# Another written-out issue order for a fused adaLN, sliding-window attention and GeGLU kernel

## The chip, the cores and the metric

The kernel runs on one core of a Trainium2 chip. Its time is device microseconds of one execution. Every engine of the core (PE for matmuls, DVE for elementwise work, ACT for activations and copies, POOL for small things, SP for issuing DMAs) has its own queue of instructions, works through it in order, and waits on semaphores for what other engines or transfers must deliver first.

## The reference, cut to what matters

The input x is 2048 rows of 512 bf16 values. Six vectors of 512 come from a conditioning vector c. They shift, scale and gate an attention layer and a feed-forward layer.

```python
mod = (silu(c) @ w_mod).reshape(1, 6, 1, 512)       # sa, ca, ga, sb, cb, gb
h = layernorm(x) * (1 + ca) + sa
x = x + ga * A(h, wqkv, wo)
h = layernorm(x) * (1 + cb) + sb
x = x + gb * (gelu(h @ w_gate) * (h @ w_up)) @ w_down    # w_gate, w_up: 512 x 1792
# A: 32 heads of 16; position s looks at s, s-2, ..., s-14 (8 places, masked below 0)
#    logits = q . k / 4, softmax over the 8 places, o = sum of attn * v, then o @ wo
```

## The kernel before, in words

**Groups.** The 2048 rows are worked on in four groups of 512 (called 0 to 3). For a group the steps are:

- LN1: statistics on DVE (L408, `bn_stats`) or ACT (L386 to L397), the inverse root on POOL (L445), the normalised rows `xn` on DVE (L422). Then `xn` is transposed: on PE for groups 0 (L481, in two halves, `th0` and `th1`), 1 and 2 (L458), by one DMA for group 3 (L464, called LN1.3.t). ACT (L496, four instructions per group, LN1.g.h0 to h3) applies scale and shift and leaves `hT`.
- qkv: twelve projections qp.g.block.j of four matmuls each (L563, L545 for the first two of group 0), each into one of four `mm` buffers of PSUM. ACT copies each out (q L577, k L579, v L583), which makes the buffer free again.
- logits: DVE multiplies q with eight shifted views of k (L618, four `pq` tiles of 128x4096). PE sums over the head dimension with 32-column tiles (L632, lp.g.0, lp.g.1, ..., and lp.g for the last). DVE and ACT do the softmax (ACT's exp is L660). The weights are brought into the layout of v by PE (L690) in group 0, and by a DMA through DRAM in the others.
- v: its transpose goes to DRAM (L589, vst.g), and four loads (L598, V4.g.0 to V4.g.2 and V4ld.g) bring shifted copies. DVE multiplies them with the weights (L725, pv.g.j), PE sums (L739, 32-column tiles), ACT copies (L750), PE multiplies with wo (L760), DVE adds x (L769).
- LN2: as LN1. Group 0 is transposed by PE, the others by DMA.
- FFN: for 14 tiles of 128 features, PE computes gate and up (L788, `g` and `u`, four matmuls each), ACT applies gelu (L821, `gl`) and copies (L828, `ub`), DVE multiplies (L839, `hh`). Then PE multiplies with w_down (L800; L811 for the last 128 rows), DVE adds x (L846, L853), and SP stores the output.

Ahead of the groups stand loads, the conditioning vectors (L294, function `cols`: 16 matmuls with one moving column each; L347 in 32-column tiles for the two gates), and twenty "warm" matmuls (L211) of a tile of zeros into a PSUM buffer that nobody reads. The gates ga and gb are spread over all partitions by a small store and a load through DRAM (L308, L312), and are multiplied into wo and w_down.

**What sets the order.** Every step is a Python generator, called a thread; it yields one `Op` after another: an engine, and a function that emits the instructions of this op. 111 threads are spawned. A list `ORDER` at the top of the file (L19 on) holds 846 thread numbers, and `Issuer.run` goes through it and emits the next op of the thread named:

```python
nxt = [next(g, None) for g in self.threads]
for i in ORDER:
    op = nxt[i]
    assert all(name in self.done for name in op.after), (op.fire, op.after)
    ...
    op.fn()
    ...
    nxt[i] = next(self.threads[i], None)
```

The list thus sets the order of every engine's queue: 276 ops on PE, 219 on DVE, 256 on ACT, 12 on POOL, 83 on SP. No scheduler changes it later (`tc.manual_schedule`). Within one thread the order is that of the code. The numbers `w` and `lat` in an `Op` are not read by `run`. Buffers come from pools (`mm` 4, `att` 2, `prod` 4, `hh` 16, and so on), and an op that takes a buffer waits on the chip until its last reader is done. Thread numbers: 0 constants, 1 to 4 loads, 5 and 6 the gates' way through DRAM, 7 and 9 to 11 the conditioning vectors, 8 the warm matmuls, 12 and 13 the gates into the weights, and from 15 on 24 per group (group 0: 15 to 38, group 1: 39 to 62, and so on; 14 is a second part of group 0's LN1).

All DMAs but two small early ones are issued by SP, and so lie on one queue.

Of the kernel before, what the change touches and what calls it, by code (L numbers as in the profile page):

```python
# [16 lines left out]
PT_DMA = (1, 2, 3)  # L17

ORDER = [  # L19
# [33 lines left out]
]  # L53


# [865 lines left out]
```

## Time and profile before

| | |
|---|---|
| median of 3 runs | 239.58 us (239.35 to 239.76) |
| span of the profiled execution | 237.6 us |
| the profiled execution's own time | not given by the page; the median lies 1.98 us above the span |
| PE, DVE, ACT busy | 231.6, 169.6, 150.7 us |
| granted PE clock | 1.00 in all stages looked at |
| DMA | 29.68 MB, 125 GB/s on average |

The span runs from the first instruction to the last. "Busy" counts the time in which an engine has an instruction under way; matmuls are pipelined, so a busy PE may still have small steps between its instructions. In a line of the timeline the first two numbers are start and length in us, then come the engine, the source line, the operation, output and input, and in brackets the idle time before it and who ended it. Source lines are those of the kernel before; the changed file is one line shorter above the functions, so its lines are lower by one.

### The profile page before, as it was taken

How to read it: one execution, taken by the hardware profiler on the slowest of the kernel's cores; microseconds unless marked ns; L12 is line 12 of the kernel's file. 1: busy time of each engine (PE TensorE's matmuls, PEld its weight loads, DVE VectorE, ACT ScalarE, POOL GpSimd, SP SyncE). 2: the span in 40 equal slices, each digit the busy share in tenths (PEclk: the TensorE clock that was granted, in tenths of full speed). 3: DMA queues.
4: the chain of work that ended last, by engine and by line, in shares of the span. 5: the costliest groups of instructions: out<-in, count | busy, mean ns of one | idle time of the engine just before them, and what ended most of it. 6: DMA issues, size and time to landing. Idle time of an engine off the chain costs nothing.

```text
span 237.6 us, 3691 instructions
## 1 busy us (share of the span) xinstructions
PE 231.6 (97%) x1403; PEld 109.1 (46%) x1403; DVE 169.6 (71%) x238; ACT 150.7 (63%) x287; POOL 12.4 (5%) x37
## 2 busy tenths in 40 slices
PE   7999899999999999999999999999999999999994
PEld 2656355544544444444444444444444444444443
DVE  3989999999999989999797899936742202322222
ACT  4689999977995756973775953552378560366300
POOL 1620101000100000010000010000100000000000
PEclk9999999999999999999999999999999999999999
DMA  6998896999967879307301977100080000100011
GB/s 213 349 306 237 219 202 162 205 356 308 193 163 211 263 181 196 59 3 177 90 0 43 206 158 136 44 22 0 22 91 1 0 22 25 44 0 0 0 47 44
DMA packets 35337, 29.68 MB, mean 125 GB/s; under 512 B 12664, under 2 KB 33784, under 8 KB 35320
## 3 DMA queue, kind: packets, MB, share of 16 engines
q1 hardware_dynamic: 35040, 29.19, 50.3%
q10 hardware_dynamic: 280, 0.26, 0.3%
q8 instruction: 11, 0.18, 0.3%
q14 instruction: 6, 0.05, 0.1%
HBM read 22.37 MB, written 4.98 MB: 115 GB/s over the span
## 4 chain that ended last, share of the span: by engine, by line
PE 87%; ACT 8%; DMA 2%; DVE 1%; issue 0%; POOL 0%; ACTq 0%
PE u_ps L788 21%; PE g_ps L788 20%; PE y_ps L800 19%; PE qkv_ps L563 12%; PE x_ps L760 6%; PE o_ps L739 3%; PE LTp L632 2%; DMA x<-in_A_x_dram 2%; ACT vT L583 2%; ACT gl L397 2%; ACT gl L386 2%; PE y_ps L811 1%; ACT hT L496 1%; PE qkv_ps L545 1%; ACT kT L579 1%; DVE st L408 1%
## 5 line engine op out<-in xcount | busy, mean ns | idle before, releaser
L788 PE MATMUL u_ps<-h,Wu 128*128 128x512 bf16 x224 | 57.6, 379 | 0.0
L788 PE MATMUL g_ps<-h,Wg 128*128 128x512 bf16 x224 | 57.5, 379 | 0.0
L821 ACT ACTIVATE gl<-g_ps 128x512 bf16<-128x512 f32 x56 | 33.7, 602 | 23.0 <-PE g_ps L788 20.8
L828 ACT CAST ub<-u_ps 128x512 bf16<-128x512 f32 x56 | 33.0, 588 | 22.6 <-PE u_ps L788 22.2
L800 PE MATMUL y_ps<-Wd,hht 128*128 128x512 bf16 x210 | 46.3, 379 | 0.0
L563 PE MATMUL qkv_ps<-hT,wqkv 128*128 128x512 bf16 x184 | 41.8, 380 | 0.6 <-ACT qT L577 0.6
L839 DVE TENSOR_TENSOR hht<-gl,ub 128x512 bf16<-128x512 bf16 x56 | 22.4, 423 | 27.1 <-ACT ub L828 27.1
L618 DVE TENSOR_TENSOR pq<-qT,kT 128x4096 bf16<-128x4096 bf16 x16 | 36.2, 2286 | 0.9 <-ACT kT L579 0.9
L725 DVE TENSOR_TENSOR pv<-PT,V 128x4096 bf16<-128x4096 bf16 x16 | 35.8, 2287 | 0.2 <-issue 0.2
L788 PEld LDWEIGHTS <-Wu 128*128 128x128 bf16 x224 | 21.4, 98 | 27.6 <-issue 2.5
L788 PEld LDWEIGHTS <-Wg 128*128 128x128 bf16 x224 | 21.7, 98 | 26.8 <-issue 1.0
L800 PEld LDWEIGHTS <-hht 128*128 128x128 bf16 x210 | 20.5, 98 | 24.8
L563 PEld LDWEIGHTS <-wqkv 128*128 128x128 bf16 x184 | 20.3, 114 | 20.3 <-issue 3.3
L846 DVE TENSOR_TENSOR ot<-y_ps,x 128x512 bf16<-128x512 f32 x15 | 10.1, 688 | 18.7 <-PE y_ps L800 18.7
L769 DVE TENSOR_TENSOR x<-x_ps,x 128x512 bf16<-128x512 f32 x16 | 10.6, 685 | 9.6 <-PE x_ps L760 9.6
L445 POOL TENSOR_TENSOR rstd<-rstd,neghalf 128x4 f32<-128x4 f32 (+1 forms) x9 | 8.6, 956 | 157.8 <-DVE rstd L439 87.3
L760 PE MATMUL x_ps<-woP,oT 128*128 128x512 bf16 x64 | 15.3, 379 | 0.0
L408 DVE BATCH_NORM_STATS2 st<-x 128x6 f32<-128x512 bf16 x19 | 12.8, 675 | 3.0 <-DMA x<-in_A_x_dram 3.0
L496 ACT ACTIVATE h<-h,modT,scl 128x512 bf16<-128x512 bf16 x12 | 8.9, 805 | 8.9 <-DMA h<-xn 8.9
L750 ACT CAST oT<-o_ps 128x512 bf16<-128x512 f32 x16 | 8.8, 591 | 7.5 <-PE o_ps L739 7.5
L579 ACT CAST kT<-qkv_ps 128x512 bf16<-128x512 f32 x16 | 9.8, 613 | 0.8 <-PE qkv_ps L563 0.8
L577 ACT CAST qT<-qkv_ps 128x512 bf16<-128x512 f32 x16 | 9.5, 604 | 0.5 <-PE qkv_ps L563 0.5
(78 smaller groups left out, 178.8 us busy)
## 6 DMA issues: line engine op xcount, KB each, us to landing
V<-vscr SPq DMA_DIRECT2D x12, 520.0 KB, 8.2
wm<-in_w_mod_dram SPq DMA_DIRECT2D x6, 512.0 KB, 4.8
vscr<-vT SPq DMA_DIRECT2D x4, 512.0 KB, 4.2
out_dram<-ot SPq DMA_DIRECT2D x15, 128.0 KB, 1.7
Wg<-in_B_w_gate_dram SPq DMA_DIRECT2D x1, 1792.0 KB, 8.9
Wu<-in_B_w_up_dram SPq DMA_DIRECT2D x1, 1792.0 KB, 12.3
wqkv<-in_A_wqkv_dram SPq DMA_DIRECT2D x3, 512.0 KB, 8.0
x<-in_A_x_dram SPq DMA_DIRECT2D x3, 512.0 KB, 9.0
```

The source lines that it names most:

```text
L408: nc.vector.bn_stats(out=st[:], in_=src()[:, c4, :])
L496: nc.scalar.activation(out=o, in_=B[key, dtp][:, :, dd, :] if pe else o, func=ACT.Identity, scale=sc(dt), bias=bi(dt))
L563: nc.tensor.matmul(ps[:], lhsT=wqkv[blk][:, dt, j::4], rhs=B["hT", sg][:, :, dt, :], start=(dt == 0), stop=(dt == DT - 1))
L579: nc.scalar.copy(out=kT[:, j, 16 + sg * SG:16 + (sg + 1) * SG], in_=ps[:])
L618: nc.vector.tensor_tensor(out=pq[:], in0=_ap(B["qT", sg][:, j, :], [[0, W], [1, SG]]), in1=_ap(kT[:, j, sg * SG + 2:sg * SG + 2 + SG], [[2 ...
L725: nc.vector.tensor_tensor(out=t[:], in0=_ap(B["PT", sg][:, 0, :], [[SG, 2], [0, 4], [1, SG]]), in1=_ap(v[:, 0, j, :], [[8, 2], [4 * (SG + ...
L760: nc.tensor.matmul(ps[:], lhsT=B["oT", sg][:, j, c4 * P:(c4 + 1) * P], rhs=woP[:, j, :], start=(j == 0), stop=(j == 3))
L788: nc.tensor.matmul(ps[:], lhsT=Wt[:, dt, ft * P:(ft + 1) * P], rhs=B["h2T", sg][:, :, dt, :], start=(dt == 0), stop=(dt == DT - 1))
L800: nc.tensor.matmul(ps[:], lhsT=B["hh", sg, ft][:, c4 * P:(c4 + 1) * P], rhs=B["Wd", ft // 4][:, ft % 4, :], start=(ft == 0), stop=(ft == F ...
L821: nc.scalar.activation(out=gl[:], in_=B["g", sg, ft][:], func=ACT.Gelu_apprx_tanh)
L828: nc.scalar.copy(out=ub[:], in_=B["u", sg, ft][:])
L839: nc.vector.tensor_tensor(out=hh[:], in0=B["gl", sg, ft][:], in1=B["ub", sg, ft][:], op=ALU.mult)
```

## The change

Only the list `ORDER` differs: 52 lines become 51, with the same 846 entries in another order. Each engine has the same ops as before, at other places in its queue. The diff begins so, and nothing outside the list is touched:

```diff
 ORDER = [
-    1, 1, 2, 2, 2, 0, 8, 8, 8, 8, 8, 17, 8, 8, 8, 8, 7, 7, 7, 7, 8, 8, 8, 8, 8, 8, 17, 17, 17, 17, 17, 17, 17,
-    17, 17, 17, 9, 17, 8, 8, 7, 7, 8, 8, 7, 7, 18, 18, 19, 19, 2, 2, 2, 2, 2, 19, 14, 14, 14, 14, 2, 2, 14, 8,
-    8, 39, 39, 39, 3, 3, 20, 20, 20, 20, 21, 21, 21, 21, 2, 2, 2, 20, 20, 20, 21, 21, 0, 0, 21, 20, 20, 20, 20,
...
+    0, 8, 8, 8, 8, 2, 17, 17, 8, 1, 1, 8, 0, 8, 17, 17, 17, 17, 8, 8, 17, 2, 2, 2, 2, 2, 2, 2, 2, 7, 7, 8, 8, 8,
+    8, 8, 7, 7, 7, 17, 17, 17, 18, 7, 7, 17, 17, 18, 7, 14, 19, 19, 0, 8, 8, 8, 8, 8, 19, 8, 8, 14, 14, 3, 3,
+    39, 39, 39, 14, 14, 2, 2, 20, 20, 20, 21, 9, 20, 41, 2, 21, 21, 20, 41, 41, 21, 21, 20, 20, 20, 20, 63, 63,
...
 ]
```

Read by engine, it moves these (before, then after):

```
PE, start:  16 warm, cols(1), 2 warm, cols(0), th0, th1, 2 warm, qph.0 (first projection)
            13 warm, cols(1), th0, cols(0), th1, 7 warm, qph.0
SP, middle: V4.0.0 V4.0.1 V4.0.2 vst.1 V4ld.0 LN1.3.t ga Wg vst.2 Wu V4.1.0
            V4.0.0 gst2 V4.0.1 V4.0.2 vst.1 ga V4ld.0 Wg LN1.3.t Wu vst.2 V4.1.0
SP, later:  pt.1.1 wm5 Wd0 Wd1 Wd2 Wd3 gst5 vst.3 gb V4.2.0
            pt.1.1 vst.3 wm5 Wd0 gst5 gb V4.2.0 Wd1 Wd2
```

In the logits sum of group 0, the last piece (lp.0) stands behind three projections of group 1 on PE, and the statistics of LN1.2 stand ahead of group 0's fourth product (L618) on DVE. The projections of group 1 come in the order in which ACT copies them out. Runs of 32-column tiles on PE are broken into 16 places where they were in 14. On PE the order from the fourth feature tile of the last group to the end is the same.

59 rows, old and new, of the table ORDER are left out of this document.

## The prediction

> **What bounds the kernel now.** The page's first part says which engine is full, its clock row whether it runs at full speed, the waits what TensorE (PE) still waits for.
>
> ```profile
> PE 231.6 (97%) x1403; PEld 109.1 (46%) x1403; DVE 169.6 (71%) x238; ACT 150.7 (63%) x287; POOL 12.4 (5%) x37
> PEclk9999999999999999999999999999999999999999
> PE 87%; ACT 8%; DMA 2%; DVE 1%; issue 0%; POOL 0%; ACTq 0%
> PE LTp L632 <- DVE pq L618: 0.8, 1, 0.8
> PE qkv_ps L563 <- ACT qT L577: 0.6, 2, 0.4
> ```
>
> PE is busy for 231.6 of 237.6 us. In the timeline its last wait of the body ends at 35.76 us; from there to the last projection it never stops. So a new order can gain only what PE loses before 35.76 (stalls, and stand-in "warm" matmuls ahead of the first real one), and loses whenever PE has to wait later. PE's timeline shows both places:
>
> ```profile
> 7.44 0.59 PE L211 MATMUL warm_ps<-gB 128*128 128x512 bf16 x2
> 8.41 1.89 PE L481 MATMUL hTp<-ident,xn 128*128 128x128 bf16 x16
> 10.13 0.59 PE L211 MATMUL warm_ps<-gB 128*128 128x512 bf16 x2
> 10.56 1.91 PE L545 MATMUL qkv_ps<-hT,wqkv 128*128 128x256 bf16 x16
> ...
> 25.17 0.61 PE L632 MATMUL LTp<-pq,Mph 128*32 128x512 bf16 x8 [0.78 <-DVE pq L618]
> 29.80 1.89 PE L563 MATMUL qkv_ps<-hT,wqkv 128*128 128x512 bf16 x8 [0.43 <-ACT qT L577]
> 35.76 2.75 PE L563 MATMUL qkv_ps<-hT,wqkv 128*128 128x512 bf16 x12 [0.18 <-ACT qT L577]
> ```
>
> Third, SP's timeline (which DMA is issued when) and the windows, for one stage where the change puts transfers in another order:
>
> ```profile
> 40.15 1.87 SPq L464 DMA_TRANSPOSE hT<-xn  x1
> 42.07 1.14 SPq L312 DMA_DIRECT2D gB<-gscr  x1
> 43.26 0.45 SPq L217 DMA_DIRECT2D Wg<-in_B_w_gate_dram  x1
> 48.94 1.55 SPq L217 DMA_DIRECT2D Wu<-in_B_w_up_dram  x1
> ```
>
> ```profile
> 39.70:41.40 1.70, 1.70 (x17) 0.83 (x9) 1.70 (x3) 1.70 (x5) 0.00 (x0) 1.00 0.00 0
> 41.40:44.10 2.70, 2.70 (x14) 1.46 (x13) 2.70 (x2) 2.48 (x5) 0.00 (x0) 1.00 1.04 202
> 46.00:50.00 4.00, 4.00 (x37) 1.75 (x36) 4.00 (x3) 4.00 (x8) 0.00 (x0) 1.00 1.02 382
> ```
>
> The last two columns are the busy share of the 16 DMA engines and GB/s. They idle from 39.7 to 41.4, then the transpose of group 3's normalised rows (LN1.3.t) fills all of them for 2.7 us, and Wg, the gate weight, follows. Each big load fills the queue until it is through.
>
> The page gives no time of its own for the profiled execution. The median of the runs, 239.58, lies 1.98 us above its span of 237.6; I keep that rest fixed, so a change of the span is added to 239.58.
>
> **The change part by part.** The instructions are the same; only their places differ. I followed the new order of each engine with start times and durations of the instructions in the trace of before. All instants are in before's clock.
>
> *Prologue.* Before: cols(1) at 7.04, two warm matmuls, cols(0), the sixteen transposes th0 and th1 (to 10.13), two warm ones, then the first projection (L545) at 10.56. After: thirteen warm matmuls, cols(1), th0, cols(0), th1, seven warm ones, the projection. The thirteenth warm matmul ends its step at 6.39, and wm1, which cols(1) needs, lands at 6.44, as before. th0 waits for its rows to 8.36, cols(0) comes behind it (to 9.12 + 0.41 = 9.53), and th1 ends at 10.13 as before, since its rows come last. Then seven warm matmuls; warm ones at full clock start 0.216 us apart: 10.13 + 7 x 0.216 = 11.64. cols(0) being 1.1 us later delays the shift and the first half of hT, ready by some 10.9, under cover of the warm matmuls. The projection starts 11.64 − 10.56 = **+1.08** later, and PE being the bound, nothing gives it back by itself.
>
> *Stalls that go.* Counted from the starts and steps of neighbouring matmuls, PE's idle time between the first projection and 35.76 is 0.17 + 0.95 + 0.60 + 0.34 = 2.06 us (the timeline puts 0.78 + 0.43 + 0.18 = 1.39 of it down to a releaser; I take the whole): a small one in group 0; the last logits sum of group 0 (L632, waits for DVE's fourth pq); two projections of group 1 that wait for PSUM which ScalarE has not yet emptied. In the new order the statistics of LN1.2 stand ahead of that pq on DVE, PE has three projections of group 1 before the logits sum, and ScalarE empties PSUM in PE's own order. What is late next is lp.1.1, behind its pq: +0.13. **−2.06 + 0.13**.
>
> *Switches between tile shapes.* Runs of 32-column tiles (L632, L739, L690, L347) between 128-column work cost a little at each edge. In the chain eight L739 matmuls behind projections take 0.55 us, behind L632 0.43, and the eight projections after them 1.85 instead of 1.73: 0.12 + 0.11 = 0.23 per excursion. The new order has 16 excursions for 14: 2 x 0.23 = **+0.46**. The other bound is nothing, if the edge is a cost of the record alone.
>
> *SP's queue.* Before: the four V4 loads of group 0, LN1.3.t, ga (the gate of the first residual, L312), Wg, vst.2, Wu. After: ga ahead of the fourth V4 load, then **Wg, then LN1.3.t**, Wu, vst.2. The V store of group 0 is issued about 1.0 later; ga puts 1.1 to 1.7 us (its issue; its share of the window behind the transpose) ahead of the fourth V4 load. The V4 stream, which ends at 39.7 before, ends at 41.3 to 42.4. pv.0.0 on DVE, naturally at 42.4, loses at most 0.7, and its consumer on PE is movable work behind other projections: nothing on PE. Wg's issue waits for nothing now, so its 1,792 KB follow at once: 1.835 MB at 382 GB/s is 4.8 us; from its first free moment behind ga (46.0) to its share of the landing at 52.16, 5.6. It is through at 46.1 to 48.0. LN1.3.t can be issued from 42.9 (its last row on DVE), behind Wg, and needs 2.7 us and 0.4 to land: 49.2 to 51.1. ScalarE would come to LN1.3.h0 (L496, four taking 2.93) at 49.1, so that PE has hT at its first projection of group 3 at 52.15, with 0.1 us to spare. PE's stall: from 0.1 to 2.0, and the middle, **+1.0**, is taken. Behind the waiting L496 on ScalarE stand copies that empty PSUM, so other PE work can't fill the hole. Wu comes later too, but it has some 7 us before its first use at 69.3 (landing 61.23 before). The transposes of LN2.1 to LN2.3 keep 1.2 to 1.6 us of room, and Wd1 to Wd3, now behind a V4 load, arrive before the down projection: nothing. If the rooms were gone, each would cost its excess.
>
> *The other joints.* From group 1's projections on, the new order starts several PE pieces as their input comes, with less than 0.15 us of room: qp.1.0.0, lp.3, g.0.0, g.1.1, u.1.3, y.1.0.1. The room is smaller than the spread of durations of a kind (a ScalarE copy takes 0.57 to 0.67). Nothing to 0.5; taken **+0.2**. PE's tail has the same order.
>
> Sum: +1.08 − 2.06 + 0.13 + 0.46 + 1.0 + 0.2 = **+0.8**, so the span goes to 238.4 and the time to **240.4 us**.
>
> **The rivals.**
>
> *The transpose is in time.* Landing by 49.1 costs nothing; later, every microsecond costs one. For it speaks that Wg at 382 GB/s and a V4 stream delayed by the low end make 49.2. Against: in before the transpose held all engines (1.04 of 16), so it finds no free one beside Wg. Then the sum is −0.39 and, with joints from 0 to 0.2, 239.2 to 239.4; if the two excursions cost nothing either, 238.7. This is the case that ends not slower. [...]
>
> *The clock falls back in the prologue.* Between 6.39 and 10.13, 3.74 us, PE now has no wide matmul, only one-column matmuls (L294) and transposes; the longest such stretch before was 2.1. At the start of before, the first warm matmuls come 0.427 us apart for about 4.3 us, then 0.216. If the clock fell, seven warm ones cost 7 x 0.21 = 1.5 more and the remaining 1.3 us at half rate 0.65: 240.4 + 2.1 = 242.5. Against: PE does not idle all that time. [...]
>
> *Another joint fails.* DVE runs 1.1 us later than before from its first pq (14.9) to the 40s, and ScalarE with it; a joint that I took for covered, at the price of that lag, gives 240.4 + 1.0 = 241.4.
>
> **How the numbers follow.** The forecast has 0.48, the transpose in time 0.25, the clock 0.10, another joint 0.17. A measurement can tell about 0.2%, 0.48 us, from no change. Faster by more is below 239.1: half of the second case and a little of the first and last, 0.18. Same, 239.1 to 240.06: the other half, a quarter of the forecast's own range (239.3 to 241.7: stall 0.1 to 2.0, joints 0 to 0.5) and a little of the last, 0.26. Slower: 0.56. The range is 238.7 (in time, switches free) to 242.3 (just short of the full price of the clock).
>
> **What would show it.** In the trace of after: the first projection at 11.6 with seven warm matmuls before it 0.22 us apart (0.43 would be the clock); no wait of L632 on pq at 25; in the waits a PE wait for hT (L496) of about 1.0 at the first projections of group 3, and ScalarE's L496 released by the DMA of hT; Wg landing ahead of hT. The forecast is wrong if Wg is through by 46, if seven warm matmuls were replaced by waiting anyway, or if PE shows waits of a kind not listed here.

## The result and the profile after

The changed kernel takes 242.55 us (median of 4 runs, 242.12 to 243.59), the kernel before beside it 239.47. The ratio is 1.0138 (95% interval 1.0114 to 1.0163): slower by 3.1 us, where 240.4 was forecast, with a range up to 242.3. The profiled execution took 242.12 with a span of 240.1, 2.5 more than the span before.

The page of the changed kernel: busy times, the clock row, the chain by engine, and PE's waits.

```profile
PE 233.0 (97%) x1403; PEld 109.5 (46%) x1403; DVE 169.8 (71%) x238; ACT 152.8 (64%) x287; POOL 15.1 (6%) x37
PEclk9799999999999999999999999999999999999999
PE 79%; DVE 13%; POOL 2%; issue 2%; DMA 2%; ACT 0%; ACTq 0%; DVEq 0%
```

```profile
PE hTp L480 <- DVE xn L421: 1.5, 1, 1.5
PE PTp L689 <- DVE e L675: 0.8, 1, 0.8
PE o_ps L738 <- DVE pv L724: 0.4, 1, 0.4
```

Three things are new. The second slice of the clock row has a 7. The waits at 25.2, 29.8 and 35.8 are gone, as forecast, but PE waits for the softmax (L689) and for a pv product (L738), which it did not before. And DVE, 1% of the chain before, is 13% of it now, with POOL behind it. PE's wait for hT of group 3, forecast at 1.0, is not there.

The start of PE's queue in the timeline after, and the windows of the same stretch, first after, then before (behind the busy times of the five engines stand the granted clock, the share of the DMA engines and GB/s):

```profile
8.34 1.11 PE L480 MATMUL hTp<-ident,xn 128*128 128x128 bf16 x8 [1.52 <-DVE xn L421]
9.24 0.61 PE L293 MATMUL modT_ps<-scT,wm 128*128 128x1 bf16 x16
9.71 1.01 PE L480 MATMUL hTp<-ident,xn 128*128 128x128 bf16 x8
10.52 2.54 PE L210 MATMUL warm_ps<-gB 128*128 128x512 bf16 x7
12.89 1.91 PE L544 MATMUL qkv_ps<-hT,wqkv 128*128 128x256 bf16 x16
```

```profile
6.30:8.30 2.00, 0.51 (x17) 0.42 (x16) 1.90 (x7) 0.54 (x3) 0.44 (x2) 1.00 1.10 352
8.30:10.50 2.20, 2.07 (x32) 1.94 (x33) 1.45 (x5) 0.58 (x2) 1.88 (x9) 0.62 1.10 349
10.50:12.50 2.00, 2.00 (x9) 0.78 (x7) 1.97 (x6) 1.94 (x7) 0.66 (x3) 0.56 1.10 349
```

```profile
8.30:10.50 2.20, 1.89 (x28) 1.30 (x26) 1.91 (x7) 1.49 (x4) 1.93 (x15) 1.00 1.09 348
10.50:12.50 2.00, 2.00 (x19) 1.86 (x17) 1.97 (x6) 1.59 (x5) 1.68 (x8) 1.00 1.10 349
```

The clock stood at half from 8.85 to 12.26 us. Windows cut at these instants show it (PE's busy time is the second number; at 5.43 the steps of the first warm matmuls go from 0.427 to 0.216 us):

```profile
5.43:8.85 3.42, 1.81 (x26) 0.97 (x25) 2.67 (x9) 1.41 (x3) 1.51 (x3) 1.00 1.08 351
8.85:12.26 3.41, 3.41 (x36) 2.31 (x34) 2.91 (x8) 2.31 (x7) 1.99 (x10) 0.50 1.09 348
```

The two halves of the transposes take 0.9 and 0.8 us from start to next start, and the first five of the seven late warm matmuls start 0.43 apart. The first projection starts at 12.89 instead of 10.56: 2.33 later. If the place costs the 1.08 that was worked out, the clock cost the other 1.25.

The chain of waits after, from 27 to 54 us, in order of time (start, length, what), shows the second part:

```profile
27.22 2.99 POOL rstd L444
30.23 1.38 DVE xn L421 x4
31.61 0.20 DVE LTp L643
...
38.69 1.22 DVE e L675
39.91 1.89 DVE pq L617
...
42.27 1.92 POOL rstd L444
...
52.12 2.29 DVE pv L724
54.46 0.62 PE o_ps L738 x8
```

From group 0's first product at 17.26 to the last pv product at 54.4 the chain runs over DVE and POOL alone. In the kernel before it ran over ACT and, from 35.76 on, over PE. DVE has two holes in this stretch, of 0.9 us each, and both end with POOL's inverse root. POOL's rows in the timeline, after and then before:

```profile
27.22 2.98 POOL L444 TENSOR_TENSOR rstd<-rstd,neghalf 128x4 f32<-128x4 f32 x1 [11.56 <-DVE rstd L438]
42.27 1.91 POOL L444 TENSOR_TENSOR rstd<-rstd,neghalf 128x4 f32<-128x4 f32 x1 [12.07 <-DVE rstd L438]
```

```profile
27.08 1.01 POOL L445 TENSOR_TENSOR rstd<-rstd,neghalf 128x4 f32<-128x4 f32 x1 [11.87 <-DVE rstd L439]
35.51 1.01 POOL L445 TENSOR_TENSOR rstd<-rstd,neghalf 128x4 f32<-128x4 f32 x1 [7.42 <-DVE rstd L439]
```

The same instruction takes 2.98 and 1.91 us instead of 1.01. In the new order DVE runs a wide product meanwhile: L617 (128x4096) from 27.05 to 29.33, and the scaling of wo (L368, 128x2048, 1.22 us) from 42.09. POOL ends 0.87 us after each. Before, DVE ran the mask and the maximum (26.91 to 28.46) and the last step of the softmax (35.36 to 36.58) at those moments.

### The profile page after: what moved, and what is told of

It is laid out like the page before. It is cut to its first block, busy times and chain, and to the rows that moved or that the text cites. A ratio compares the mean times of both kernels' runs of the same rounds, so it can differ in the third digit from the quotient of the medians.

```text
span 240.1 us, 3700 instructions
## 1 busy us (share of the span) xinstructions
PE 233.0 (97%) x1403; PEld 109.5 (46%) x1403; DVE 169.8 (71%) x238; ACT 152.8 (64%) x287; POOL 15.1 (6%) x37
## 4 chain that ended last, share of the span: by engine, by line
PE 79%; DVE 13%; POOL 2%; issue 2%; DMA 2%; ACT 0%; ACTq 0%; DVEq 0%
PE u_ps L787 20%; PE g_ps L787 20%; PE y_ps L799 19%; PE x_ps L759 6%; PE qkv_ps L562 5%; DVE pq L617 4%; PE o_ps L738 3%; DVE pv L724 2%; POOL rstd L444 2%; DMA x<-in_A_x_dram 2%; PE LTp L631 2%; DVE xn L421 2%; PE y_ps L810 1%; DVE st L407 1%; PE warm_ps L210 1%
## 5 line engine op out<-in xcount | busy, mean ns | idle before, releaser
L617 DVE TENSOR_TENSOR pq<-qT,kT 128x4096 bf16<-128x4096 bf16 x16 | 36.2, 2285 | 2.8 <-ACT kT L578 2.8
L444 POOL TENSOR_TENSOR rstd<-rstd,neghalf 128x4 f32<-128x4 f32 (+1 forms) x9 | 11.4, 1271 | 162.6 <-DVE rstd L438 82.7
L495 ACT ACTIVATE h<-h,modT,scl 128x512 bf16<-128x512 bf16 x12 | 8.8, 804 | 12.3 <-DMA h<-xn 12.3
L768 DVE TENSOR_TENSOR x<-x_ps,x 128x512 bf16<-128x512 f32 x16 | 10.5, 675 | 1.6 <-PE x_ps L759 1.6
```

Source lines behind the costliest of these rows:

```text
L444: nc.gpsimd.tensor_tensor(out=k["rstd"][:, a:b], in0=k["rstd"][:, a:b], in1=neghalf[:, a:b], op=ALU.pow)
L617: nc.vector.tensor_tensor(out=pq[:], in0=_ap(B["qT", sg][:, j, :], [[0, W], [1, SG]]), in1=_ap(kT[:, j, sg * SG + 2:sg * SG + 2 + SG], [[2 ...
L768: nc.vector.tensor_tensor(out=x[:, c4, :], in0=B["x1ps", sg, c4][:], in1=x[:, c4, :], op=ALU.add)
```

## The experiments

`G` below is the changed kernel with five warm matmuls moved (a_warm_gap); later edits start from it. An edit is written as the change in one engine's queue.

### The clock at the start

Five of the late warm matmuls go into the wait ahead of the transposes:

```diff
 PE: 13 warm, cols(1)
+    5 warm
     th0, cols(0), th1
-    7 warm
+    2 warm
     first projection
```

> The changed kernel, with five of the seven late warm matmuls moved ahead of th0, into the wait for its rows; two stay behind th1. Clock theory (the first projection came 2.3 us late because PE's clock fell to half in a stretch without wide matmuls, and because the late warm matmuls stood in its way): the granted clock stays 1.00, th0 and th1 take about 0.5 us each again instead of 0.9 and 0.8, the first projection starts at 10.6, and the time falls by the whole 2.3 us, to about 240.2. Rival (the clock falls because PE waits for rows and then transposes, whatever stands in the wait): the clock still falls near 8.3, the first projection starts near 11.8, and the time is about 241.4.

240.39 (10 runs, 240.03 to 240.83; before beside it 239.56, ratio 1.0007, 0.9974 to 1.004). The medians lie 0.8 us apart; the ratio takes in four executions of the kernel before whose clock fell, and its interval includes 1. All ten executions of G have a mean granted clock of 0.998 to 1.000; in the six kernels below that share this start, the clock fell in 3 of 58 executions. Its timeline:

```profile
7.07 1.24 PE L210 MATMUL warm_ps<-gB 128*128 128x512 bf16 x5
8.87 0.89 PE L480 MATMUL hTp<-ident,xn 128*128 128x128 bf16 x8 [0.56 <-DVE xn L421]
9.60 0.54 PE L293 MATMUL modT_ps<-scT,wm 128*128 128x1 bf16 x16
11.03 2.21 PE L544 MATMUL qkv_ps<-hT,wqkv 128*128 128x256 bf16 x16
```

The gain is 2.2 of the expected 2.3, or 2.0 against the second measurement of the changed kernel below (rows came 0.5 us later in this execution, so that its first projection starts at 11.03, not 10.6). The clock theory holds, its rival falls.

The reverse, the kernel before with the new start of PE's queue alone:

```diff
-PE: 16 warm, cols(1), 2 warm, cols(0), th0, th1, 2 warm, first projection
+PE: 13 warm, cols(1), th0, cols(0), th1, 7 warm, first projection
```

> The kernel before, with only the start of PE's queue as in the changed kernel (13 warm, cols(1), th0, cols(0), th1, 7 warm). Clock theory: the granted clock falls to about 0.6 between 8.3 and 12.3, the first projection starts at 12.9, PE's later waits stay, and the time is 239.5 + 2.3 = 241.8. Rival (the start costs only its place, 1.1 us, and the rest comes from the waits further on): 240.6, with the clock at 1.00. Second rival (DVE and ACT catch up): less than 240.3.

242.37 (10 runs; ratio 1.009, 1.0051 to 1.0129). In the profiled execution the clock is 0.69 on average from 8.3 to 10.5 and 0.50 from 10.5 to 12.5, and the first projection starts at 12.93. PE's three old waits are all there (0.8 at L632, 0.6 at L563). Nine of the ten executions have a mean clock of 0.993 or 0.986; the tenth, at 1.000, took 240.28, which is 0.7 above the kernel before; the place alone was worked out at 1.08. So the start is worth some 2.8 us by the medians (2.2 by the ratio), most of the change's 3.1.

Meant as cols(0) ahead of th0:

> The changed kernel, with cols(0) ahead of th0 instead of behind it, so that PE's idle wait ahead of th0 is cut from 1.5 us to about 1.0. If what counts is the stretch without wide matmuls (3.7 us from the last warm one to th1's end): the clock falls all the same, and the time stays near 242.5. If what counts is PE's idle time: the clock stays at 1.00, the late warm matmuls run at 0.22 us each, the first projection starts at 11.6, and the time is about 241.3.

The moved entry of the list named a thread whose next op was another one, an ACT copy, so the order on every engine stayed that of the changed kernel. The run is a second measurement of it: 242.37 (10 runs, ratio 1.009, 1.0046 to 1.0133), and a useful one. Two executions kept the clock (mean 1.000) and took 240.74 and 240.84; six at 0.993 took 241.98 to 242.65; two at 0.986 took 243.29 and 244.10. The changed kernel at full clock is thus a 240.8 us kernel; a fall costs 1.6 us, one of twice the loss in the mean clock 2.9. The true edit:

```diff
 PE: 13 warm, cols(1)
+    cols(0)
     th0
-    cols(0)
     th1, 7 warm, first projection
```

> The changed kernel with cols(0) truly ahead of th0 on PE (in a_cols_first the moved entry of the list only emitted an ACT copy of the same thread, so that every engine's order stayed that of the changed kernel). PE's idle wait ahead of th0 is then cut into two, of about 0.9 and 0.4 us, while the stretch without wide matmuls, 3.7 us, stays. If that stretch is what counts: the clock falls in most executions all the same, and the median stays at 242.0 to 242.6. If PE's idle time counts: the clock stays at 1.00 in most, the first projection starts at 11.6, and the median is 240.7 to 240.9.

242.75 (5 runs; before 239.26; ratio 1.0148, 1.0133 to 1.0164), all five at 0.993 or 0.986. PE was busy for 1.22 of the 2.00 us from 6.3 to 8.3, against 0.51 in the changed kernel, and the clock fell all the same, at 8.99:

```profile
5.57:8.99 3.42, 2.54 (x44) 1.70 (x42) 2.85 (x9) 1.47 (x5) 1.74 (x5) 1.00 1.09 352
8.99:12.40 3.41, 3.04 (x15) 1.63 (x15) 2.99 (x10) 3.17 (x8) 1.76 (x8) 0.50 1.10 349
```

So a shorter idle wait did not keep the clock up: PE waits 0.72 us ahead of cols(0) here, where the changed kernel waits 1.52 ahead of th0, and all five executions fell. PE's busy time ahead of the fall is 1.81 of 3.42 us in the changed kernel and 2.54 of 3.42 here; the clock fell after both. In both traces the half clock lasts 3.41 us, behind 3.42 us at 1.00. In those of b_gap, a_cols_first and a_no_late_warm it lasts 3.4 us as well, as an estimate from what the clocks of the windows 8.3 to 10.5, 10.5 to 12.5 and 12.5 to 14 lack of 1.00 (0.69, 0.50, 0.98; 0.57, 0.62, 1.00; 0.64, 0.54, 1.00). What these five traces share is a long stretch without a wide matmul (256 or 512 columns), by PE's rows 4.1 to 4.8 us, part of it at half clock (6.39 to 10.52 in the changed kernel, 6.46 to 10.65 here). It is 2.5 us in G and 2.1 in the kernel before, and their traces show no fall. With five warm matmuls inside the stretch the clock stayed up in all ten executions of G and in 55 of 58 of the six kernels below; one of the other three is the profiled one of g_stats_wos_t (0.993). At which length it falls, and why the same program falls in some executions and not in others, no run shows.

The seven late warm matmuls left out:

```diff
-    pl.spawn(warmup(13, 20))
+    pl.spawn(warmup(13, 13))
```

(Their seven entries leave the list too.)

> The changed kernel without the seven late warm matmuls (thirteen in all; they are work that nobody reads). If the clock comes back some 4 us after it fell, whatever matmuls PE runs meanwhile: the first projection starts near 10.9 at half clock, the clock is full again near 12.3, 0.7 us of projection is done by then, and the time falls by 1.2 us, to about 241.3. Rival (the projections of 256 columns wake the clock later than the warm matmuls of 512): the slow stretch lasts longer and the time is 242.5 or more.

241.83 (10 runs, 241.00 to 243.38; ratio 1.008, 1.0044 to 1.0117), every execution with a fallen clock. The first projection starts at 11.07, and the clock is 0.64 on average from 8.3 to 10.5, 0.54 from 10.5 to 12.5 and 1.00 after. So the clock came back under real projections (an estimated 3.4 us at half, by those windows) as it did under warm matmuls (3.41), and without them PE gains some work in the slow stretch. The gain is about half of the expected 1.2, 0.5 against the second measurement above and 0.7 against the first: the direction of the first theory, not its size.

### Who makes PE wait later

The product of group 0 that POOL ran beside goes ahead of LN1.2's statistics:

```diff
 DVE: pq.0.2
+     pq.0.3
      LN1.2 statistics
-     pq.0.3, LN1.2 rows, mask, maximum, subtraction
+     mask, maximum, subtraction, LN1.2 rows
 PE:  two projections of group 1
+     lp.0
      third projection
-     lp.0
```

> Compared with the kernel that has five warm matmuls in the wait ahead of th0 (a_warm_gap, 240.4), whose other orders are those of the changed kernel. Here group 0's fourth product (L617) stands ahead of LN1.2's statistics on DVE, the rows of LN1.2 behind the subtraction (L654), and the last logits sum one projection earlier on PE. POOL theory (the root of LN1.2 on POOL took 2.98 us instead of 1.01 because DVE ran the wide bf16 product meanwhile, and DVE then waited 0.9 us for it, so that PE waits 0.9 for the softmax at L689): POOL's root takes 1.0 again, DVE's wait of 0.9 goes, PE's wait at L689 falls below 0.2, and the time falls by about 0.9 to 239.5. Rival (DVE simply has too much to do ahead of the softmax): the wait at L689 stays at 0.9 and the time at 240.4.

241.55 (11 runs; before 239.46; ratio 1.0076, 1.0048 to 1.0103): 1.2 slower than G, where 0.9 faster was expected. POOL's row and DVE's product in the timeline:

```profile
30.42 1.01 POOL L444 TENSOR_TENSOR rstd<-rstd,neghalf 128x4 f32<-128x4 f32 x1 [14.02 <-DVE rstd L438]
```

```profile
26.16 2.29 DVE L617 TENSOR_TENSOR pq<-qT,kT 128x4096 bf16<-128x4096 bf16 x1 [1.89 <-ACT kT L578]
```

The root takes 1.01 us again, as the POOL theory says. But the product now stands open for 1.89 us, waiting for k: the new order also put the last k projection of group 0 behind the first logits sums and transposes (20.25 before, 24.98 after), as filler in the place where PE waited before. The statistics had covered that hole. DVE ends the softmax no sooner, PE waits 0.9 at L689 as in G, and 0.9 more at L631, where I had moved lp.0 ahead of its product. (This profiled execution also waited 1.2 for the first block of w_mod, at 7.4, which is no part of the edit.) So the run says nothing on the price of POOL's delay.

The other place:

```diff
 DVE: LN1.3 root's input
-     scaling of wo
      LN1.3 rows, four pv products
+     scaling of wo
```

> a_warm_gap with the multiplication of wo by the gate (L368) moved on DVE from ahead of LN1.3's rows to behind the fourth pv product, where the kernel before has it. POOL theory: POOL's root of LN1.3 takes 1.0 instead of 1.9 us, the rows and the pv products come 0.9 earlier, PE's wait on the fourth pv product (0.5 us at L738) goes, and 0.5 us is gained, to 239.9, if hT of group 3 is in time; its transpose would still lie behind Wg, and if it now ends last, PE waits for L495 instead and the gain is 0 to 0.2. Rival (POOL is slow there for another reason): root 1.9, no gain, or a loss of up to 0.3 because x1 comes later.

240.68 (12 runs; ratio 1.0043, 1.0022 to 1.0065), no gain on G. POOL's root takes 1.01 us here too, and PE's wait at L738 is gone. But DVE still has nothing else to do while it waits for the root, and 1.22 us of scaling now stand ahead of group 1's last product; PE waits 0.5 there:

```profile
PE PTp L689 <- DVE e L675: 0.9, 1, 0.9
PE LTp L631 <- DVE pq L617: 0.5, 1, 0.5
```

The cost by itself, then: the root of LN1.2 and LN1.3 is left out, and a short DVE instruction stands for it, right behind the root's input and ahead of the wide product (L617) or the scaling of wo (L368). For this an entry of the list moves too.

```diff
-            nc.gpsimd.tensor_tensor(out=k["rstd"][:, a:b], in0=..., in1=neghalf[:, a:b], op=ALU.pow)
+            if ev in ("LN1.2", "LN1.3"):
+                nc.vector.tensor_scalar(out=k["rstd"][:, a:b], in0=k["rstd"][:, a:b], scalar1=1.0, scalar2=None, op0=ALU.mult)
+            else: ...
```

> a_warm_gap without the inverse root of LN1.2 and LN1.3 on POOL: a short DVE instruction of the same small tile stands in its place, and the root is left out, so the rows of groups 2 and 3 are scaled by the variance instead. It measures what DVE's two waits for POOL cost. If they are what makes PE wait at L689 (0.9) and L738 (0.5): both waits go, and the time falls by 1.3 to 1.5, to about 239.0; if hT of group 3 then ends last (its transpose lies behind Wg), PE waits up to 0.6 at its first projection of group 3, and the time is 239.5. Rival (DVE is late for its amount of work, not for POOL): 240.2 to 240.4.

239.02 (12 runs, 238.28 to 240.42; before 239.40; ratio 0.9978, 0.9955 to 1.0001): 1.4 below G, as the POOL theory had it (1.2 if each is taken against the kernel before beside it, since G was not run again here). All that is left in the list of PE's waits:

```profile
PE warm_ps L210 <- DVE gB L205: 1.2, 1, 1.2
PE hTp L483 <- DVE xn L421: 0.3, 1, 0.3
PE LTp L634 <- DVE pq L620: 0.2, 1, 0.2
```

The waits on the softmax and on pv are both gone with DVE's two holes. The hT of group 3 now ends last, and costs 0.16: PE's second projection of group 3 starts that much late.

### The transpose and Wg

```diff
 SP: V4ld.0
-    Wg, LN1.3.t
+    LN1.3.t, Wg
     Wu, vst.2
```

> a_warm_gap with LN1.3.t ahead of Wg in SP's queue, as in the kernel before. By the step of the prediction (the transpose behind Wg costs PE 1.0): the time falls to about 239.4. By the trace of the changed kernel (the transpose lands 2 us later than it would alone, but PE comes to group 3 later still): nothing, 240.4, with hT landing about 2 us earlier.

241.80 (6 runs; before 239.46; ratio 1.0105, 1.0057 to 1.0154): 1.4 slower than G (1.0 among the executions at full clock). Neither the prediction's step (1.0 faster) nor the rival (no change) had the sign. The windows, first of G, then of this kernel (last two columns: share of the 16 DMA engines, GB/s), and the new wait:

```profile
39.70:41.40 1.70, 1.70 (x20) 0.48 (x18) 1.70 (x3) 1.70 (x5) 0.62 (x1) 1.00 1.05 267
41.40:44.10 2.70, 2.70 (x14) 1.40 (x13) 1.80 (x6) 2.70 (x7) 1.29 (x1) 1.00 1.03 400
```

```profile
39.70:41.40 1.70, 1.70 (x20) 0.61 (x14) 1.61 (x3) 1.70 (x4) 1.14 (x1) 1.00 0.02 6
41.40:44.10 2.70, 2.70 (x14) 1.46 (x13) 1.89 (x5) 2.70 (x6) 0.77 (x1) 1.00 0.00 0
```

```profile
PE gR_ps L346 <- DMA wm<-in_w_mod_dram: 1.1, 1, 1.1
```

With the transpose ahead, Wg stands behind a DMA that waits for DVE, and the 16 engines idle from 39.7 to 44.1. Everything behind it on SP's queue comes later: group 2's v is stored at 61.0 instead of 56.9, the load of group 1's softmax weights is issued at 72.2 instead of 70.7, the last block of w_mod (wm5) at 75.4 instead of 73.9, and PE, which needs that block for the second gate (L346), waits 1.1 us for it, until 80.5. The new place of Wg, which I had priced as a loss, is a gain in this order.

The same exchange without the roots:

> The same, with LN1.3.t ahead of Wg in SP's queue. The difference to g_noroot is the price of the transpose behind Wg once DVE is in time: 0.3 to 1.0 by the prediction's step, nothing if the transpose is hidden anyway. The time: 238.9 to 239.2.

240.69 (11 runs, 239.27 to 241.61; before 239.40; ratio 1.0049, 1.0030 to 1.0068): 1.7 slower than g_noroot. The 0.16 at group 3 goes, and PE waits 1.3 for wm5 and 0.5 on a pv product of group 1 instead. The three edits together, on G:

> All three edits on a_warm_gap together. If the gains add (0.9 for the softmax, 0.5 for pv, nothing or a little for the transpose): 239.0, about 0.4 below the kernel before, and PE has no wait over 0.2 us behind its first projection. If a third resource takes the place of the two waits (DVE is busy without a hole from 27 to 62 us): 239.6 or more.

242.12 (6 runs; before 239.46; ratio 1.0101, 1.0062 to 1.0140). Nothing adds: PE has the waits of all three (1.2 at L631, 0.9 at L689, 0.5 for wm5). This profiled execution also has a fallen clock (0.993), so only its waits are used here, and not its time.

### What PE's old waits were worth

The kernel before, with one of ACT's pieces of work moved as in the changed kernel:

```diff
 ACT: LN1.3 first three sums
-     LN1.3 fourth sum, mean, first square
      three copies of group 1's projections
+     LN1.3 fourth sum, mean, first square
```

> The kernel before, with one edit: on ACT the last sum, the mean and the first square of LN1.3 (L386, L392, L397) go behind the first three copies of group 1's projections, as in the changed kernel, so that PE need not wait 0.6 and 0.3 us for PSUM at 29.8 and 35.8. If PE alone sets the end (the prediction's step, by which a stall of PE that goes is a gain): 0.6 to 0.9 less, 238.6 to 238.9. If DVE is a second bound up to 55 us (it runs without a hole from 15 to 55, and its fourth pv and last pq product end 0.2 and 0.1 us before PE wants them): PE waits the same time later, at L739 and L632, and the time stays at 239.3 to 239.5.

239.43 (12 runs; before 239.40; ratio 1.0015, 0.9984 to 1.0046): no change. PE's waits in this kernel:

```profile
PE qkv_ps L563 <- ACT qT L577: 0.9, 1, 0.9
PE LTp L632 <- DVE pq L618: 0.8, 1, 0.8
```

The wait at 29.8 is gone, and the one at 35.8 has grown from 0.34 to 1.02 us by the steps of its matmuls: 0.94 before, 1.02 now. The time stayed where the second theory had it, but not for its reason: it is ACT, not DVE, that hands the wait on. Whether DVE would have caught a real gain (its last product of group 1 ends 0.1 us before PE wants it in the kernel before) was not reached.

No version here that computes everything is faster than the kernel before; G comes within 0.8 us by the medians.

## Why the prediction was wrong, point by point

Step by step, from the start times of PE's matmuls in the two profiled executions (that of the changed kernel is the fastest of its four). The fifth row holds what the others leave of the total:

| step | forecast | measured |
|---|---|---|
| prologue, by place | +1.08 | +1.08, taken as worked out (0.7 in the one execution of b_gap at full clock) |
| prologue, by the clock | 0 (a rival, 0.10) | +1.25, the rest of 2.33 |
| old stalls | −2.06 | −2.06 |
| lp.1.1 behind its product | +0.13 | +0.13 |
| tile switches and other joints | +0.66 | +0.67 |
| hT of group 3 behind Wg | +1.0 | 0 |
| softmax late at L689, pv late at L738 | 0 | +0.87 + 0.59 |
| sum | +0.8 | +2.53 |

- **Prologue.** "The projection starts 11.64 − 10.56 = +1.08 later" is the step that failed: it took seven warm matmuls at 0.216 us each. Four of their steps took 0.427. I had the fallen clock as a rival at 240.4 + 2.1 = 242.5, and argued that "PE does not idle all that time"; a_cols_early shows that this is no argument (the clock fell with PE busy for 2.54 of the 3.42 us ahead of it), and the measured median is that rival's time. That the two agree is luck: the rival holds 2.1 for the clock and 1.0 for hT, which came as 1.25 and 0, and lacks the 1.46 at L689 and L738. The fall was named and its chance was far too small: the changed kernel fell in all four of its executions and in eight of ten of its repeat. Its size is 1.6 us in the medians of whole runs, not 2.1. The mean clocks come in steps of 0.007 of some 240 us, which is 1.7 us of full clock or 3.4 us at half, as the traces have it (3.41).
- **Stalls that go.** Right on PE, all four are gone, and worth less than that: the filler that removed the wait at 25.2 is the last k projection of group 0, which DVE then gets 2.4 us later against the rest of its work. The order hid that hole under the statistics of LN1.2, and by this put the wide product beside POOL's root. I had listed both moves; the prediction goes by the durations of the trace of before, in which the root takes 1.01 us and not 2.98.
- **pv on DVE**, "nothing on PE", and the rival "another joint fails" at 241.4: this rival came true as well, at L689 and L738, with 1.46 us. Its cause is POOL, and not the lag that the rival named. That the root grows beside a wide DVE product is shown by both moves (2.98 and 1.91 us become 1.01 each); that DVE's two waits cost the kernel 1.2 to 1.4 us is shown by g_noroot. By the trace the two slow roots end 0.87 us after L617 and L368, which had started 0.17 and 0.18 us before them; beside the mask, the maximum and the last softmax step the root takes 1.01 in the kernel before. Why it is slow beside the two products, no run shows.
- **SP's queue.** The order came as worked out: Wg's bytes from about 42 to 46 us, the transpose behind them. But it was not Wg alone that set the transpose's time. DVE ended its rows at 45.6 (worked out: 42.9), SP issued it at 45.66, and it landed at 51.9 (forecast 49.2 to 51.1), 6.3 us after its issue where it took 4.4 before. ScalarE's four L495 then ended at 54.88, and PE came to group 3 at 55.0 and not at 52.15, because of the start and of its two waits for DVE. So the late transpose cost nothing here, by 0.1 us and with the help of the other delays; with DVE in time it costs 0.16. What was missing is the other side: the idle time of the 16 engines from 39.7 to 41.4, which I showed, and which Wg fills.
- **Switches, joints, tail.** What is left for them is within 0.1 of the forecast, and the list of PE's waits after names no single joint of mine.

The range ended at 242.3, just short, because it was built to stop ahead of "the full price of the clock" and no case in it held two rivals at once. They are not exclusive: the clock's 1.25 and DVE's 1.46 lie in different stages, and add.

Even without the fall the forecast was near for the wrong reasons. At full clock the changed kernel takes 240.8, 1.3 above the kernel before, where 0.8 was forecast: the 1.0 for hT, which did not come, stands against the 1.46 at L689 and L738, which was not forecast. Behind the start, gains and losses nearly cancel.

## What to carry to other kernels

An order that is tight on the bounding engine moves its slack to the engines that feed it: follow every one of them, POOL too, through the stage where their work has no holes, and look at which two run side by side (here POOL's root took 2.98 us beside a DVE product, and 1.01 without). Put stand-in matmuls into a stretch in which PE has only one-column matmuls, transposes and waits, not behind it: here such a stretch of 4.1 us went with 3.41 us at half clock, though PE was busy for 1.81 of the 3.42 us ahead of the fall, and five warm matmuls inside it kept the clock at 0.998 to 1.000 in all ten executions of G. A large load that waits for nothing belongs ahead of a transfer that waits for an engine, if the queue would idle meanwhile: with Wg behind the transpose the 16 engines idled from 39.7 to 44.1 us, and the kernel was 1.4 us slower.

## What the runs showed of the hardware

- The granted clock stood at half for 3.41 us in the traces of the changed kernel (8.85 to 12.26) and of a_cols_early (8.99 to 12.40), both times behind 3.42 us at 1.00. The five traces with a fall among the kernels without G's start have 4.1 to 4.8 us without a wide matmul ahead of the projections; those of G, with 2.5, and of the kernel before, with 2.1, have no fall.
- The clock fell in some executions of a program and not in others: the changed kernel in its repeat ran with a mean of 1.000, 0.993 or 0.986, at 240.8, 242.4 and 243.7 us. The kernel before, whose longest stretch without wide matmuls is 2.1 us, fell too, in 4 of 31 executions beside the first experiments (0.991 to 0.993, 241.3 to 242.2 us).
- POOL's inverse root of a 128x4 tile took 1.01 us, 2.98 beside a DVE product of 2.28 us (L617), and 1.91 beside one of 1.22 (L368), which had each started just before it. It ended 0.87 us after the product both times.
- The clock came back after 3.41 us at half under warm matmuls (the changed kernel), and after an estimated 3.4 us under real projections (a_no_late_warm).
